# Shrunk spectra stored in six residue classes where PSUM is read, forward spectra turned on chip for every batch

## Chip, core and metric

The kernel runs on one core of a Trainium2 chip. The metric is the device time of one execution in microseconds (us), lower is better; the median over runs counts. Matrix products run on TensorE (PE; its weight loads are listed apart as PEld), element-wise work on VectorE (DVE), ScalarE (ACT) and GpSimd (POOL); SyncE (SP) issues most DMAs. [...]

## What is computed

Three parts in a row. First, for 8 batches of a sequence of 3072 rows by 256 columns, a spectral layer; then a soft mixture of 8 experts with 4 slots each over all 24576 rows; then a feed-forward layer.

```python
X = np.fft.rfft(x, axis=1)                      # 8 batches
Yr = Xr @ w_r - Xi @ w_i + b_r
Yi = Xr @ w_i + Xi @ w_r + b_i
Yr = np.sign(Yr) * np.maximum(np.abs(Yr) - 0.01, 0.0)   # "shrunk" spectra
Yi = np.sign(Yi) * np.maximum(np.abs(Yi) - 0.01, 0.0)
y = np.fft.irfft(Y, n=3072, axis=1)
...
logits = x @ phi                                # x is y, 32 slots
d = exp(logits - logits.max(0)); d /= d.sum(0) + 1e-9
slot_input = d.T @ x                            # through relu(. @ w1) @ w2 per expert
c = exp(logits - logits.max(1)); c /= c.sum(1) + 1e-9
x = c @ slot_out
...
h = x @ w_in
out = (h * tanh(softplus(h))) @ w_out
```

## The kernel before

The rows y are never formed. Since the slots are linear in y, the kernel projects the shrunk spectrum on phi, turns the 32 projected columns back by an inverse transform to get the logits, makes the weights d, transforms d forward, and sums spectrum times transformed weights. The inverse and forward transforms are split in two steps each (64 by 48 points).

The front part (up to about 645 us) works in 32 steps, four for each batch b; step k = 4b+g treats a quarter of the spectrum, all 256 channels in two halves `h` (input) or `eh` (output). In one step:

- `load_b` brings the result of the first transform step from DRAM, `stage2` does the second transform step in PSUM (tile `s`), ACT rounds it to a high part `xh`, DVE takes the low part `xl`.
- `linear` multiplies with the three weight combinations a, b, c (m = 0, 1, 2; six products each half, tile `l`). For m = 0 ACT copies PSUM to `k1`. For m = 1 and 2 (real and imaginary part) DVE adds `k1` to PSUM, giving `p`; ACT makes `cl` and overwrites `p` (two Relu with bias); POOL subtracts the two into `yt`, the shrunk spectrum. `cl` has one buffer, `p` two, `yt` two.
- `project` (tile `pp`) and `inv1` (tile `iu`) begin the logits. `ytrans` turns `yt` with 12 products against the identity (tile `tr`, with `yt` as the stationary operand), and ACT copies the result to `y`.

Once for each batch: `sturn`, `inv2` (`lps`), `smax1` to `smax3` (running maximum and exponent, tiles `mt`, `mb`, `dx`), `fwd1` (first step of the forward transform of the weights, PSUM tile `dps`, copied to `dm`), `d_load` (brings `dm` into the order that the next step wants, tile `dd`), `fwd2` (`dt`), `dturn` (`dh`), `slots` (`sps`: sum over `y` with `dh`). In `ctrans` the combine weights c are turned (`ctps`) with a contiguous operand. `stage1` (PSUM tile `s`, copied by ACT to `a`) and `store_a` prepare the batch ahead. `conv` converts the feed-forward weights in pieces on DVE and POOL.

One layout matters. Before, `yt` holds for each output half (8 q) x (real, imaginary) x (48 f), and `ytrans` takes column 2c+i and every sixth after it, six classes m in all. `dm` and `dd`: before, for all batches but the last, ACT copies `dps` to `dm`, a DMA stores it to the DRAM tile `ddr`, and a second DMA loads it as `dd` in the new order. The last batch has a second way: two DVE transposes of 32x32 blocks out of PSUM with a stepped output, eight products with the identity (`td`), and two copies out of PSUM.

The order of the work is written by hand. Every piece is put with `at(position, ...)` on one line of positions counted in steps k, and all pieces are issued in the order of positions; each engine and each DMA queue then works strictly in that order. The constants are in the table `PA` (`dl` places `d_load`, `f1` `fwd1`, `f2` `fwd2`); the last four steps and the last batch have their own table `TAIL`. The PSUM tiles of the front part share eight buffers, given out in turn. After 690 us only the feed-forward layer `ffn` runs.

Of the kernel before, what the change touches and what calls it, by code (L numbers as in the profile page):

```python
# [8 lines left out]
F32 = mybir.dt.float32  # L9
# [12 lines left out]
NP = 32  # L22
# [9 lines left out]
def constants():  # L32

    n1 = np.arange(R1, dtype=np.float64)
    n2 = np.arange(R2, dtype=np.float64)
    f1 = np.zeros((R1, R1))
    t = np.zeros((96, NP, 96))
    w = 2.0 * np.pi / SEQ
    f1[:, 0], f1[:, 1] = 1.0, np.where(n1 % 2 == 0, 1.0, -1.0)
    for pos in range(47):  # L40
        k, r = (R1 * (pos + 1), 0) if pos < 23 else (R1 // 2 + R1 * (pos - 23), R2)
        a = w * np.mod(n2 * k, SEQ)
        t[r:r + R2, 0, pos] = np.cos(a)
        t[r:r + R2, 0, 48 + pos] = -np.sin(a)
    t[0:R2, 0, 47] = 1.0
    t[0:R2, 0, 95] = np.where(n2 % 2 == 0, 1.0, -1.0)
    for q in range(1, NP):
        ang = 2.0 * np.pi * np.mod(n1 * q, R1) / R1
        f1[:, 2 * q], f1[:, 2 * q + 1] = np.cos(ang), -np.sin(ang)
        for k2 in range(R2):  # L50
            a = w * np.mod(n2 * (q + R1 * k2), SEQ)
            sg = 1.0 if k2 < R2 // 2 else -1.0
            t[0:R2, q, k2] = np.cos(a)
            t[R2:96, q, k2] = np.sin(a)
            t[0:R2, q, 48 + k2] = -sg * np.sin(a)
            t[R2:96, q, 48 + k2] = sg * np.cos(a)
    fd = np.kron(f1, np.eye(2))
    sel = np.tile(np.eye(NS), (4, 1))
    m = np.arange(128).reshape(4, 4, 2, 4)
    order = m.transpose(1, 0, 2, 3).reshape(-1)  # L60
    big = np.concatenate([fd, fd.T[order], np.eye(128), sel, np.tile(f1, (2, 1))], axis=1)
    tt = t.transpose(2, 1, 0)
    t3 = np.concatenate([t[:, :, 0:48] + t[:, :, 48:96], t], axis=2)
    both = np.concatenate([t3.reshape(96, -1), tt.reshape(96, -1)], axis=1)
    return np.ascontiguousarray(big.astype(np.float32)), np.ascontiguousarray(both.astype(np.float32))
# [3 lines left out]
def body(ctx, tc, x, w_r, w_i, b_r, b_i, phi, w1, w2, w_in, w_out, cbig, ct, out, dbg=None, stop=False):  # L69
# [154 lines left out]
    def stage2(k, h, p0):  # L224
        b, g = divmod(k, 4)
        n = min(3, 8 - p0)
        if h == 0 and p0 == 0:
            xh_t[k] = bp.tile([128, 2, 3 * NC + 48], F32R, tag="xh", name="xh")
            xl_t[k] = bp.tile([128, 2, 3 * NC + 48], F32R, tag="xl", name="xl")
        full = psum([128, 3, 3, 48], "s2")  # L230
        ps = full[:, 0:n]
        for i in range(n):
            nc.tensor.matmul(ps[:, i], lhsT=b_t[k][:, p0 + i, h * 128:(h + 1) * 128], rhs=t_m[:, 8 * g + p0 + i, :],  # L233
                             start=True, stop=True)

        def part(t):
            return t[:, h, 144 * p0:144 * (p0 + n)].rearrange("p (q r f) -> p q r f", r=3, f=48)

        xh = part(xh_t[k])
        nc.scalar.activation(out=xh, in_=ps, func=AF.Copy)  # L240
        nc.vector.tensor_sub(part(xl_t[k]), ps, xh.bitcast(F32))  # L241
        if g == 0 and p0 == 0:
            for t in (xh_t[k], xl_t[k]):
                nc.vector.tensor_copy(t[:, h, 3 * NC:3 * NC + 48].rearrange("p (a r) -> p a r", r=2),
                                      t[:, h, 95:144:48][:, None, :].to_broadcast([128, 24, 2]).bitcast(F32))

    def linear(k, eh, m):
        if eh == 0 and m == 0:
            pool, tag = (bp, "b") if k >= NK - 2 else (yq, "yq") if k >= NK - 4 else (ytp, "yt")
            yt_t[k] = pool.tile([128, 2, 8, 2, 48], F32, tag=tag, name="yt")  # L250
        xh, xl, yt = xh_t[k], xl_t[k], yt_t[k]
        src, (wh, wl) = ((0, wsp["a"]), (2, wsp["b"]), (1, wsp["c"]))[m]
        w, nq = (NC + 2, 9) if m == 0 and k % 4 == 0 else (NC, 8)
# [11 lines left out]
                nc.tensor.matmul(full[:, 0:48 * nq].rearrange("p (q f) -> p q f", f=48), lhsT=ww[:, h, es], rhs=spec(xx, h), start=n == 0, stop=n == 5)  # L265
                n += 1
        if m == 0:
            k1_t[eh] = lp.tile([128, NC + 2], F32, tag="k1", name="k1")
            nc.scalar.activation(out=k1_t[eh][:, 0:w], in_=ps, func=AF.Copy)
            if w > NC:  # L270
                cs_t[eh] = cs = sm.tile([128, 2, 2], F32, tag="cs", name="cs")
                for i, sc in ((0, 0.5), (1, -0.5)):
                    nc.scalar.activation(out=cs[:, i], in_=k1_t[eh][:, NC:w], func=AF.Relu, scale=sc, bias=half[:, i, eh:eh + 1])
            return
        ri = m - 1
        p = lp.tile([128, 8, 48], F32, tag="p", name="p")
# [697 lines left out]
```

## Time and profile before

| What | Value |
|---|---|
| three runs | 1929.86, 1931.71, 1935.7 us; median 1931.71 |
| profiled execution, own time | 1935.8 us |
| its span (first to last instruction) | 1934.0 us |
| PE busy | 1875.3 us, 97% of the span |
| DVE, ACT, POOL busy | 1163.1, 860.5, 195.3 us |
| mean DMA share up to 600 us | about 0.6 to 0.9 of the 16 engines |
| small packets (under 512 B) | 28784 of 96905 |
| chain that ended last | PE 88%, DMA 4%, DVE 3%, ACT 2%, issue 2%, POOL 1% |

The busy time of PE includes the pipelining of products, so a busy PE may still be shortened. The rows that follow come from the profiled execution; it is 4.1 us (0.2%) above the median.

### The profile page before, as it was taken

What the parts mean: (1) busy time and instruction counts of PE and PEld (TensorE: products, weight loads), DVE (VectorE), ACT (ScalarE), POOL (GpSimd) and SP (SyncE); (2) the same over time, 40 slices, a digit from 0 to 9 for tenths busy, and PEclk for the clock granted to TensorE, in tenths of its full rate; (3) what the DMA queues carried; (4) which work ended last, traced back from release to release, by engine and by line L of the source; (5) the groups of instructions that cost most, each with busy time, mean ns of one, the idle gap of its engine ahead of it and who ended that gap; (6) DMA issues with size and microseconds to landing.
All of it is one profiled execution on the core that took longest, in us unless ns stands there. A gap on an engine that the chain in (4) does not pass through costs nothing.

```text
span 1934.0 us, 29831 instructions
## 1 busy us (share of the span) xinstructions
PE 1875.3 (97%) x12106; PEld 1569.4 (81%) x12106; DVE 1163.1 (60%) x1810; ACT 860.5 (44%) x1380; POOL 195.3 (10%) x247
## 2 busy tenths in 40 slices
PE   6899999998998899999999999999999999999999
PEld 4687787777887488888888888888888888888887
DVE  3355655655566476666666666666666666666665
ACT  2666666665754243333333333333333333333332
POOL 0333333332332000000000000000000000000000
PEclk9999999999999999999999999999999999999999
DMA  9867777775663920020020020002002001000000
GB/s 246 235 150 173 168 184 177 170 185 132 161 167 107 343 74 22 23 55 22 12 55 23 23 55 23 23 12 55 22 23 55 22 19 48 22 23 22 23 22 23
DMA packets 96905, 164.28 MB, mean 85 GB/s; under 512 B 28784, under 2 KB 58096, under 8 KB 94848
## 3 DMA queue, kind: packets, MB, share of 16 engines
q1 hardware_dynamic: 93808, 155.13, 29.2%
q0 software_dynamic: 1792, 4.76, 0.8%
q10 hardware_dynamic: 1168, 2.49, 0.5%
q8 instruction: 95, 1.56, 0.3%
q14 instruction: 42, 0.34, 0.1%
HBM read 98.78 MB, written 63.57 MB: 84 GB/s over the span
## 4 chain that ended last, share of the span: by engine, by line
PE 88%; DMA 4%; DVE 3%; ACT 2%; issue 2%; POOL 1%; SPq 0%; POOLq 0%; ACTq 0%; DVEq 0%
PE o L910 56%; PE h L868 9%; PE l L265 8%; PE s L233 6%; PE tr L318 2%; PE s L201 2%; DMA dd<-ddr 2%; DMA bt<-sdr 1%; PE pp L296 1%; DMA xc<-in_x_dram 1%; PE sps L496 1%; POOL yt L285 1%; PE dt L478 1%; ACT cl L283 1%; PE iu L307 1%
## 5 line engine op out<-in xcount | busy, mean ns | idle before, releaser
L910 PE MATMUL o<-whl,gh 128*128 128x512 f32 x3072 | 1082.9, 395 | 0.0
L910 PE MATMUL o<-whl,gl 128*128 128x256 f32 x3072 | 827.9, 280 | 0.0
L881 ACT ACTIVATE g<-h 128x1024 f32<-128x1024 f32 (+1 forms) x385 | 394.2, 1025 | 747.8 <-PE h L868 738.0
L910 PEld LDWEIGHTS o<-whl,gh 128*128 128x128 f32 x3072 | 566.5, 188 | 121.5
L910 PEld LDWEIGHTS o<-whl,gl 128*128 128x128 f32 x3072 | 578.5, 188 | 31.5
L894 DVE TENSOR_TENSOR gl<-g,gh 128x1024 fp32r<-128x1024 f32 x383 | 468.9, 1224 | 29.2 <-DVE gh L887 1.4
L887 DVE CAST gh<-g 128x1024 fp32r<-128x1024 f32 (+1 forms) x385 | 265.8, 690 | 352.6 <-ACT g L881 352.6
L868 PE MATMUL h<-ctt,mst 128*128 128x512 f32 x768 | 240.7, 394 | 1.5 <-ACT g L881 1.0
L233 PE MATMUL s<-tall,bt 96*128 96x144 f32 x1024 | 143.0, 301 | 23.0 <-DMA bt<-sdr 12.1
L233 PEld LDWEIGHTS s<-tall,bt 96*128 96x128 f32 x1024 | 138.6, 202 | 31.0 <-issue 26.4
L241 DVE TENSOR_TENSOR xl<-s,xh 128x432 fp32r<-128x432 f32 (+1 forms) x192 | 94.6, 550 | 113.6 <-ACT xh L240 113.3
L285 POOL TENSOR_TENSOR yt<-cl,p 128x384 f32<-128x384 f32 x124 | 125.2, 1010 | 352.6 <-ACT p L284 220.2
L868 PEld LDWEIGHTS h<-ctt,mst 128*128 128x128 f32 x768 | 121.0, 188 | 19.7 <-ACT g L881 1.8
L283 ACT ACTIVATE cl<-p,tup 128x384 f32<-128x384 f32 x124 | 76.3, 615 | 134.0 <-DVE p L277 98.1
L918 DVE TENSOR_TENSOR os<-o,os 128x256 f32<-128x256 f32 x192 | 76.5, 419 | 77.2 <-ACT os L917 77.2
L277 DVE TENSOR_TENSOR p<-l,k 128x384 f32<-128x384 f32 x128 | 70.6, 553 | 85.2 <-PE l L265 61.9
L240 ACT ACTIVATE xh<-s 128x432 fp32r<-128x432 f32 (+1 forms) x192 | 79.0, 503 | 36.7 <-PE s L233 36.3
L917 ACT ACTIVATE os<-o 128x256 f32<-128x256 f32 x192 | 73.4, 383 | 41.5 <-PE o L910 37.7
L284 ACT ACTIVATE p<-p,tlo 128x384 f32<-128x384 f32 x124 | 76.3, 615 | 4.0
L201 PE MATMUL s<-xc,f 64*64 64x512 f32 x384 | 56.6, 650 | 9.6 <-DMA xc<-in_x_dram 9.5
L318 PEld LDWEIGHTS tr<-cb,yt 128*128 128x128 f32 x384 | 55.4, 235 | 12.0 <-issue 4.5
L318 PE MATMUL tr<-cb,yt 128*128 128x128 f32 x384 | 62.2, 306 | 0.0
(187 smaller groups left out, 1392.1 us busy)
## 6 DMA issues: line engine op xcount, KB each, us to landing
sdr<-a SPq DMA_DIRECT2D x96, 256.0 KB, 3.8
bt<-sdr SPq DMA_DIRECT2D x32, 768.0 KB, 8.5
out_dram<-os SPq DMA_DIRECT2D x47, 512.0 KB, 2.6
xc<-in_x_dram SPq DMA_DIRECT2D x90, 256.0 KB, 5.4
ctt<-c_d SPq DMA_DIRECT2D x28, 384.0 KB, 7.0
w1t<-in_moe_w_dram SPq DMA_DIRECT2D x6, 1024.0 KB, 7.4
c_d<-chl SPq DMA_DIRECT2D x14, 384.0 KB, 2.8
w2t<-in_moe_w_dram SPq DMA_DIRECT2D x5, 1024.0 KB, 12.2
```

Of the source, the lines that this page charges most:

```text
L201: nc.tensor.matmul(ps[h][64 * c:64 * c + 64], lhsT=f64[hs], rhs=t[hs, XC * c:XC * c + XC], start=True, stop=True, tile_position=(64 * h, 6 ...
L233: nc.tensor.matmul(ps[:, i], lhsT=b_t[k][:, p0 + i, h * 128:(h + 1) * 128], rhs=t_m[:, 8 * g + p0 + i, :], start=True, stop=True)
L241: nc.vector.tensor_sub(part(xl_t[k]), ps, xh.bitcast(F32))
L265: nc.tensor.matmul(full[:, 0:48 * nq].rearrange("p (q f) -> p q f", f=48), lhsT=ww[:, h, es], rhs=spec(xx, h), start=n == 0, stop=n == 5)
L283: nc.scalar.activation(out=cl, in_=p, func=AF.Relu, bias=tup[:, ri, eh:eh + 1])
L285: nc.gpsimd.tensor_sub(yt[:, eh, :, ri, :], cl, p)
L318: nc.tensor.transpose(ps[:, i, eh], yt[:, eh].rearrange("p q r f -> p (q r f)")[:, 2 * c + i::6], ident)
L868: nc.tensor.matmul(ps[:, i], lhsT=mst[:, f * 128:f * 128 + 128], rhs=ct_t[b][:, 4 * m:4 * m + 4].rearrange("p n t -> p (n t)"), start=True ...
L881: nc.scalar.activation(out=v(g), in_=v(h), func=AF.Mish)
L887: nc.vector.tensor_copy(v(gh), v(g))
L894: nc.vector.tensor_sub(gl, g, gh.bitcast(F32))
L910: nc.tensor.matmul(o, lhsT=a[:, i, ts], rhs=w, start=f == 0 and n == 0, stop=f == 15 and n == 1)
```

## The change

1. `yt` becomes [128, 2, 6 m, 128]: for each half, six blocks of 128, one for each class m, and within a block q, then real and imaginary part, then 8 f. The reordering happens where PSUM is read: `split6` views the PSUM tile with steps of 6 elements (24 bytes), and `k1`, `p` and `cl` are held in the order m, q, f. POOL writes `yt` in runs of 8 elements where it wrote runs of 48. The transposes take 128 contiguous columns; `project` reads runs of 16 instead of 32, and the rows of the constant table `tt` are permuted to match.
2. `fwd1` and `d_load` take the on-chip way in all batches; the DRAM tile and its two DMAs go. `dl` goes from 2.05 to 2.2.
3. In the first piece of each fourth step, the two special bins are spread over 48 columns from PSUM by one ACT copy and one DVE subtraction, instead of two DVE copies after the rounding. Two small Relu (`cs`) read PSUM instead of `k1`.

The title of the change also speaks of the second stage in one block; the positions of `stage2` are the same in both versions.

```diff
-    tt = t.transpose(2, 1, 0)
+    r = np.arange(16)
+    tt = t.transpose(2, 1, 0)[np.concatenate([6 * r + m for m in range(6)])]
...
         nc.scalar.activation(out=xh, in_=ps, func=AF.Copy)
+        real = g == 0 and p0 == 0
+        if real:
+            bins = full.rearrange("p q r f -> p (q r f)")[:, 95:144:48][:, None, :].to_broadcast([128, 24, 2])
+            bh, bl = (t[:, h, 3 * NC:3 * NC + 48].rearrange("p (a r) -> p a r", r=2) for t in (xh_t[k], xl_t[k]))
+            nc.scalar.activation(out=bh, in_=bins, func=AF.Copy)
         nc.vector.tensor_sub(part(xl_t[k]), ps, xh.bitcast(F32))
-        if g == 0 and p0 == 0:
-            for t in (xh_t[k], xl_t[k]):
-                nc.vector.tensor_copy(t[:, h, 3 * NC:3 * NC + 48].rearrange("p (a r) -> p a r", r=2),
-                                      t[:, h, 95:144:48][:, None, :].to_broadcast([128, 24, 2]).bitcast(F32))
+        if real:
+            nc.vector.tensor_sub(bl, bins, bh.bitcast(F32))
+
+    def split6(t):
+        return t[:, 0:NC].rearrange("p (q f m) -> p m q f", q=8, m=6)
...
-            k1_t[eh] = lp.tile([128, NC + 2], F32, tag="k1", name="k1")
-            nc.scalar.activation(out=k1_t[eh][:, 0:w], in_=ps, func=AF.Copy)
+            k1_t[eh] = lp.tile([128, 6, 8, 8], F32, tag="k1", name="k1")
+            nc.scalar.activation(out=k1_t[eh], in_=split6(full), func=AF.Copy)
...
-        p = lp.tile([128, 8, 48], F32, tag="p", name="p")
-        nc.vector.tensor_add(p.rearrange("p q f -> p (q f)"), ps, k1_t[eh][:, 0:NC])
+        o = yt[:, eh].rearrange("p m (q r f) -> p m q r f", q=8, r=2)[:, :, :, ri]
+        p = lp.tile([128, 6, 8, 8], F32, tag="p", name="p")
+        nc.vector.tensor_add(p, split6(full), k1_t[eh])
...
-            nc.gpsimd.tensor_sub(yt[:, eh, :, ri, :], cl, p)
+            nc.scalar.activation(out=cf, in_=pf, func=AF.Relu, bias=tup[:, ri, eh:eh + 1])
+            nc.scalar.activation(out=pf, in_=pf, func=AF.Relu, scale=-1.0, bias=tlo[:, ri, eh:eh + 1])
+            nc.gpsimd.tensor_sub(o, cl, p)
...
-                nc.tensor.transpose(ps[:, i, eh], yt[:, eh].rearrange("p q r f -> p (q r f)")[:, 2 * c + i::6], ident)
+                nc.tensor.transpose(ps[:, i, eh], yt[:, eh, 2 * c + i], ident)
...
-            if last:
-                nc.vector.transpose(out=dm.rearrange("p q n -> p n q")[:, 12 * i:12 * i + 12], in_=ps)
-            else:
-                nc.scalar.activation(out=dm[:, 12 * i:12 * i + 12], in_=ps, func=AF.Copy)
...
-        ddr[b] = dram.tile([NP, 96, NS], F32, tag="ddr", bufs=2, name="ddr")
-        nc.sync.dma_start(out=ddr[b].rearrange("q (r n) s -> (q r) n s", r=4), in_=dm)
+            nc.vector.transpose(out=dm.rearrange("p q n -> p n q")[:, 12 * i:12 * i + 12], in_=ps)
+        ch[b, 0] = dm
...
     def d_load(b):
         if b < NB - 1:
-            dd = cp.tile([96, NP, NS], F32, tag="dd", name="dd")
-            nc.sync.dma_start(out=dd, in_=ddr[b].rearrange("q p s -> p q s"))
-            ch[b, 0] = [dd[:, q] for q in range(NP)]
-            return
+            both = cp.tile([96, 2, 4, 128], F32, tag="dd", name="dd")
```

On PE, in the second batch between the projection and the forward transform `dt`, this stands before:

```order
L296 MATMUL pp<-yt,ph 32x256 x6
L318 MATMUL tr<-cb,yt 128x128 x12
L265 MATMUL l<-xh,ch 128x384
L265 MATMUL l<-xl,ch 128x384
L265 MATMUL l<-xh,cl 128x384
...
L201 MATMUL s_2463<-xc,f_120 64x512 x2
L201 MATMUL s_2464<-xc,f_120 64x512 x2
L478 MATMUL dt<-tall,dd 32x16x6 x8
```

and this now:

```order
L305 MATMUL pp<-yt,ph 32x256 x6
L452 MATMUL td<-cb,dm 96x128 x8
L327 MATMUL tr<-cb,yt 128x128 x12
L272 MATMUL l<-xh,ch 128x384
L272 MATMUL l<-xl,ch 128x384
L272 MATMUL l<-xh,cl 128x384
...
L202 MATMUL s_2481<-xc,f_120 64x512 x2
L202 MATMUL s_2482<-xc,f_120 64x512 x2
L477 MATMUL dt<-tall,dd 32x16x6 x8
```

Eight `td` stand ahead of the twelve `tr`; nothing else moves on PE.

On DVE, in the same batch, around the sum `p` that is made after `dps`, before:

```order
L277 TENSOR_TENSOR p<-l,k_2283 128x384
L552 SCALAR_TENSOR_TENSOR cvc<-cvs 128x256
L277 TENSOR_TENSOR p<-l,k_2283 128x384
L241 TENSOR_TENSOR xl<-s_2344,xh 128x432
L241 TENSOR_TENSOR xl<-s_2350,xh 128x432
```

and now:

```order
L285 TENSOR_TENSOR p<-l,k_2292 128x384
L551 SCALAR_TENSOR_TENSOR cvc<-cvs 128x256
L285 TENSOR_TENSOR p<-l,k_2292 128x384
L441 STREAM_TRANSPOSE dm<-dps 128x12x32 x2
L247 TENSOR_TENSOR xl<-s_2351,xh 128x432
L247 TENSOR_TENSOR xl<-s_2357,xh 128x432
```

The two transposes `dm` stand between the sums and the low parts; on ACT the two copies `dm` are gone from ahead of the copies `a` and `xh`.

On the SP queue, in the same stretch, before:

```order
L440 DMA ddr<-dm 128x768
L216 DMA sdr<-a 128x1x512 x2
L445 DMA dd<-ddr 96x32x32
L183 DMA xc<-in_x_dram 64x1024 x2
L221 DMA bt<-sdr 96x8x256
```

and now:

```order
L217 DMA sdr<-a 128x1x512 x2
L184 DMA xc<-in_x_dram 64x1024 x2
L222 DMA bt<-sdr 96x8x256
L532 DMA cvs<-in_moe_w_in_dram 128x512
L217 DMA sdr<-a 128x1x512 x2
```

The store of `dm` and the load of `dd` are gone from the queue, and the loads behind them move up.

## Rows read from the trace of the kernel before

**Rows 1.** Busy time by stretch: PE, PEld, DVE, ACT, POOL (instructions), clock, DMA.

```profile
core 0: us, PE busy (x) PEld busy (x) DVE busy (x) ACT busy (x) POOL busy (x), PEclk, DMA share, GB/s
60.00:130.00 70.00, 62.05 (x446) 48.32 (x443) 30.92 (x72) 42.36 (x86) 21.75 (x28) 0.93 0.79 205
...
203.00:276.00 73.00, 70.59 (x605) 55.61 (x604) 44.08 (x102) 48.06 (x100) 25.09 (x32) 1.00 0.71 174
...
690.00:1934.00 1244.00, 1239.97 (x6847) 1071.42 (x6845) 783.38 (x950) 457.00 (x571) 0.00 (x0) 1.00 0.09 29
```

**Rows 2.** Waits of PE, 20 to 640 us: total us, times, longest.

```profile
PE s L233 <- DMA bt<-sdr: 12.1, 3, 6.5
PE dt L478 <- DMA dd<-ddr: 9.9, 7, 2.5
...
PE s L233 <- ACT dm L435: 2.5, 5, 0.9
PE dps L431 <- ACT dx L384: 1.8, 2, 1.2
```

**Rows 3.** Chain that ended last, 200 to 300 us: start, us, what.

```profile
231.51 6.26 DMA dd<-ddr
...
256.61 0.33 PE ctps L413 x3
...
270.80 1.82 PE tr L318 x12
```

**Rows 4.** Groups by line and form: weight loads of the transposes, busy us, mean ns.

```profile
L318 PEld LDWEIGHTS tr<-cb,yt 128*128 128x128 f32 x384 | 55.4, 235 | 12.0 <-issue 4.5 <-DVE p L277 3.3 <-DVE xl L241 2.5
...
L413 PEld LDWEIGHTS ctps<-cb,lg 128*128 128x128 f32 x48 | 5.9, 147 | 1.9 <-POOL lg L405 1.5 <-issue 0.4
```

**Rows 5.** Timeline at 638 us, the last batch's on-chip turn: start, us.

```profile
638.09 1.08 PE L453 MATMUL td<-cb,dm 128*96 128x128 f32 x8
```

**Rows 6.** Groups by form: what takes `dps` and `td` out of PSUM.

```profile
L435 ACT ACTIVATE dm<-dps 128x384 f32<-128x384 f32 x14 | 5.9, 474 | 0.0
...
L433 DVE STREAM_TRANSPOSE dm<-dps 128x384 f32<-128x384 f32 x2 | 2.1, 1152 | 0.2 <-PE dps L431 0.2
...
L456 DVE COPY dd<-td 96x512 f32<-96x512 f32 x1 | 0.7, 686 | 1.2 <-PE td L453 1.2
```

**Rows 7.** Timeline around `dm` in the second batch; in brackets idle time before.

```profile
224.63 0.55 DVE L277 TENSOR_TENSOR p<-l,k 128x384 f32<-128x384 f32 x1
...
228.75 1.49 PE L233 MATMUL s<-tall,bt 96*128 96x144 f32 x10 [0.48 <-ACT dm L435]
...
230.50 2.88 DVE L241 TENSOR_TENSOR xl<-s,xh 128x432 fp32r<-128x432 f32 x6 [5.32 <-ACT xh L240]
```

**Rows 8.** Groups by form: PSUM reads, `rm` and `mst` stepped, `p` and `a` contiguous.

```profile
L277 DVE TENSOR_TENSOR p<-l,k 128x384 f32<-128x384 f32 x128 | 70.6, 553 | 85.2 <-PE l L265 61.9 <-POOL yt L285 12.7 <-POOL yt L288 4.1
...
L207 ACT ACTIVATE a<-s 128x512 f32<-128x512 f32 x90 | 48.8, 592 | 18.5 <-PE s L201 11.8 <-DMA xc<-in_x_dram 6.5
...
L343 DVE TENSOR_REDUCE rm<-lps 128x32 f32<-128x384 f32 x16 | 8.3, 553 | 13.5 <-ACT lg L341 13.4
...
L851 ACT ACTIVATE mst<-mr 128x512 fp32r<-128x512 f32 x2 | 1.1, 595 | 1.4 <-PE mr L846 1.4
```

**Rows 9.** Groups by form: element-wise work on POOL.

```profile
L285 POOL TENSOR_TENSOR yt<-cl,p 128x384 f32<-128x384 f32 x124 | 125.2, 1010 | 352.6 <-ACT p L284 220.2 <-PE tr L318 78.9 <-ACT chl L414 14.4
...
L554 POOL TENSOR_TENSOR cvc<-cva,cvc 128x256 f32<-128x256 f32 x32 | 23.3, 729 | 17.4 <-DVE cvc L552 17.4
...
L392 POOL TENSOR_TENSOR lg<-lg,cm 128x768 f32<-128x768 f32 x1 | 1.5, 1482 | 19.4 <-DVE cm L391 19.4
```

**Rows 10.** Waits of ACT, 130 to 640 us: total us, times, longest.

```profile
ACT cl L283 <- POOL yt L285: 26.1, 24, 1.5
```

**Rows 11.** Groups by form: the two DVE copies of the special bins.

```profile
L244 DVE CAST xl<-xl 128x48 fp32r<-128x48 f32 x16 | 4.0, 247 | 0.0
...
L244 DVE CAST xh<-xh 128x48 fp32r<-128x48 f32 x16 | 3.3, 204 | 0.0
```

More of the change, by code (lines that the diff above doesn't have):

```diff
@@ L125, in body @@
     x_t, b_t, xh_t, xl_t, yt_t, y_t, pt_t, k1_t = {}, {}, {}, {}, {}, {}, {}, {}
-    sdr, spt, ddr, ch, a_t = {}, {}, {}, {}, {}
+    sdr, spt, ch, a_t = {}, {}, {}, {}
     XC = 512
@@ L249, in linear @@
             pool, tag = (bp, "b") if k >= NK - 2 else (yq, "yq") if k >= NK - 4 else (ytp, "yt")
-            yt_t[k] = pool.tile([128, 2, 8, 2, 48], F32, tag=tag, name="yt")
+            yt_t[k] = pool.tile([128, 2, 6, 128], F32, tag=tag, name="yt")
         xh, xl, yt = xh_t[k], xl_t[k], yt_t[k]
@@ L272, in linear @@
                 for i, sc in ((0, 0.5), (1, -0.5)):
-                    nc.scalar.activation(out=cs[:, i], in_=k1_t[eh][:, NC:w], func=AF.Relu, scale=sc, bias=half[:, i, eh:eh + 1])
+                    nc.scalar.activation(out=cs[:, i], in_=full[:, NC:w], func=AF.Relu, scale=sc, bias=half[:, i, eh:eh + 1])
             return
         ri = m - 1
-        p = lp.tile([128, 8, 48], F32, tag="p", name="p")
-        nc.vector.tensor_add(p.rearrange("p q f -> p (q f)"), ps, k1_t[eh][:, 0:NC])
-        cl = lp.tile([128, 8, 48], F32, tag="cl", bufs=1, name="cl")
+        o = yt[:, eh].rearrange("p m (q r f) -> p m q r f", q=8, r=2)[:, :, :, ri]
+        p = lp.tile([128, 6, 8, 8], F32, tag="p", name="p")
+        nc.vector.tensor_add(p, split6(full), k1_t[eh])
+        cl = lp.tile([128, 6, 8, 8], F32, tag="cl", bufs=1, name="cl")
+        pf, cf = (t.rearrange("p m q f -> p (m q f)") for t in (p, cl))
         if k == NK - 1:
-            nc.vector.tensor_scalar(cl, p, tlo[:, ri, eh:eh + 1], thi[:, ri, eh:eh + 1], op0=ALU.max, op1=ALU.min)
-            nc.vector.tensor_sub(yt[:, eh, :, ri, :], p, cl)
-        else:
-            nc.scalar.activation(out=cl, in_=p, func=AF.Relu, bias=tup[:, ri, eh:eh + 1])
-            nc.scalar.activation(out=p, in_=p, func=AF.Relu, scale=-1.0, bias=tlo[:, ri, eh:eh + 1])
-            nc.gpsimd.tensor_sub(yt[:, eh, :, ri, :], cl, p)
+            nc.vector.tensor_scalar(cf, pf, tlo[:, ri, eh:eh + 1], thi[:, ri, eh:eh + 1], op0=ALU.max, op1=ALU.min)
+            nc.vector.tensor_sub(o, p, cl)
+        else:
+            nc.scalar.activation(out=cf, in_=pf, func=AF.Relu, bias=tup[:, ri, eh:eh + 1])
+            nc.scalar.activation(out=pf, in_=pf, func=AF.Relu, scale=-1.0, bias=tlo[:, ri, eh:eh + 1])
+            nc.gpsimd.tensor_sub(o, cl, p)
         if m == 2 and k % 4 == 0:
             cs = cs_t.pop(eh)
-            nc.gpsimd.tensor_sub(yt[:, eh, 0, :, 47], cs[:, 0], cs[:, 1])
+            nc.gpsimd.tensor_sub(yt[:, eh, 5, 7:16:8], cs[:, 0], cs[:, 1])
     def project(k):
@@ L293, in project @@
         for eh in range(2):
-            v = yt[:, eh].rearrange("p q r f -> p q (r f)")
+            v = yt[:, eh].rearrange("p m (q j) -> p q m j", q=8)
             for a in range(3):
-                nc.tensor.matmul(ps[32 * a:32 * a + 32], lhsT=ph[:, eh, :], rhs=v[:, :, 32 * a:32 * a + 32],
+                nc.tensor.matmul(ps[32 * a:32 * a + 32], lhsT=ph[:, eh, :], rhs=v[:, :, 2 * a:2 * a + 2],
                                  start=eh == 0, stop=eh == 1, tile_position=(0, 32 * a))
@@ L427, in fwd1 @@
         last = b == NB - 1
-        dm = cp.tile([128, 32, N2] if last else [128, N2, NS], F32, tag="st" if last else "chl", bufs=1 if last else 2, name="dm")
+        dm = cp.tile([128, 32, N2], F32, tag="st" if last else "chl", bufs=1 if last else 2, name="dm")
         for i in range(2):
@@ L431, in fwd1 @@
             nc.tensor.matmul(ps, lhsT=f1, rhs=d[:, 12 * i:12 * i + 12], start=True, stop=True)
-            if last:
-                nc.vector.transpose(out=dm.rearrange("p q n -> p n q")[:, 12 * i:12 * i + 12], in_=ps)
-            else:
-                nc.scalar.activation(out=dm[:, 12 * i:12 * i + 12], in_=ps, func=AF.Copy)
-        if last:
-            ch[b, 0] = dm
-            return
-        ddr[b] = dram.tile([NP, 96, NS], F32, tag="ddr", bufs=2, name="ddr")
-        nc.sync.dma_start(out=ddr[b].rearrange("q (r n) s -> (q r) n s", r=4), in_=dm)
+            nc.vector.transpose(out=dm.rearrange("p q n -> p n q")[:, 12 * i:12 * i + 12], in_=ps)
+        ch[b, 0] = dm
     def d_load(b):
         if b < NB - 1:
-            dd = cp.tile([96, NP, NS], F32, tag="dd", name="dd")
-            nc.sync.dma_start(out=dd, in_=ddr[b].rearrange("q p s -> p q s"))
-            ch[b, 0] = [dd[:, q] for q in range(NP)]
-            return
+            both = cp.tile([96, 2, 4, 128], F32, tag="dd", name="dd")
         src = ch[b, 0].rearrange("p (c r) n -> p c (r n)", r=4)
@@ L453, in d_load @@
                 nc.tensor.transpose(ps[:, c], src[:, 4 * a + c], ident)
-            dd = yp.tile([96, 4, 128], F32, tag="y", name="dd")
+            dd = both[:, a] if b < NB - 1 else yp.tile([96, 4, 128], F32, tag="y", name="dd")
             if a:
@@ L795, in run @@
                 nc.vector.tensor_copy(sot[:, h, 16 * g:16 * g + 16].rearrange("p (j i) -> p j i", i=SPE), src)
-PA = dict(y=20, s1=-5.89, s1d=0.3402, lb=-1.91, s2=-1.1, s2d=0.0002, pj=1.18, yt=2.24, ytd=0.0002, tu=0.482, i2=1.17, m1=1.17, m2=1.34, m3=1.51, f1=1.84, c1=1.58, ce=1.58, ds=2.47, dl=2.05, c2=2.57, f2=2.46, sl=3.2, rc=0.3, cx=3.24, cxd=0.0002, x0=-0.79, x1=0.05, ytl=1.05, x2=1.3, x3=2.7)
+PA = dict(y=20, s1=-5.89, s1d=0.3402, lb=-1.91, s2=-1.1, s2d=0.0002, pj=1.18, yt=2.24, ytd=0.0002, tu=0.482, i2=1.17, m1=1.17, m2=1.34, m3=1.51, f1=1.84, c1=1.58, ce=1.58, ds=2.47, dl=2.2, c2=2.57, f2=2.46, sl=3.2, rc=0.3, cx=3.24, cxd=0.0002, x0=-0.79, x1=0.05, ytl=1.05, x2=1.3, x3=2.7)
 TAIL = {
```

## Prediction

> **What bounds the kernel now.** I read the busy time by stretch first [rows 1]. After 690 us PE is busy 1240.0 of 1244 us with the feed-forward layer, which the change does not touch; all gain or loss lies before that. In a typical stretch of the front part (203 to 276 us, about one batch) PE is busy 70.6 of 73 us, DVE 44.1, ACT 48.1, POOL 25.1, the DMA engines 71%. So the front part too is bound by PE, and what counts is PE's own work and the few microseconds in which it waits. From 60 to 130 us it is not so: PE is idle 8 us there, and the longest wait for a load of `bt`, 6.5 us [rows 2], falls in it; work saved there is partly lost again.
>
> Next come the waits of PE [rows 2]. Two of the four matter here: `dt` waits 7 times, 9.9 us in all, for the load of `dd`, and `stage2` waits 5 times, 2.5 us, until ACT has copied `dm` and so freed a PSUM buffer. The first load of `bt` (12.1 us, three times) is early and untouched. `dps` waits 1.8 us for the exponent.
>
> Then the chain that ended last [rows 3]. It shows the load of `dd` with 6.26 us in that batch, and on PE a group of twelve `tr` in 1.82 us, 0.152 us each. Three `ctps`, the same 128x128 transpose but with a contiguous operand, take 0.33 us, 0.110 us each. The weight loads say where the difference sits: 235 ns for the stepped `yt`, 147 ns for the contiguous operand [rows 4].
>
> **The change part by part.**
>
> *Transposes with contiguous operands.* 32 steps with 12 each: 384 transposes, from 0.152 to 0.110 us by the rows of [rows 3], 12 x 0.042 = 0.50 us a step. The lower bound is no gain at all, if the 0.152 is not due to the step of 24 bytes; the upper is 32 x 0.50 = 16 us. The row nearest in kind, same engine, same shape, same stretch, is `ctps`, so I take 0.110. The first three steps' transposes run where PE is idle for loads anyhow [rows 1]; 29 x 0.50 = **-14.5 us**.
>
> *No trip of `dm` through DRAM.* The wait of `dt` goes, **-9.9 us** [rows 2]. What is late next: `dd` now needs `td` and two copies. After `td` PE still has twelve `tr`, six `l` and four products of `stage1` ahead of `dt`, about 3.4 us, and the copies take 0.69 us on DVE [rows 6] and 0.59 us on ACT (the 128x512 copy `a` of [rows 8] is the same length), so `dt` should not wait. The wait of `stage2` for `dm` goes too, **-2.5 us** [rows 2], if DVE empties `dps` earlier than ACT did. In the second batch DVE ends its sum `p` at 225.18 us [rows 7]; two transposes of 1152 ns [rows 6] end at 227.5 us, and the product that waited stands at 228.75 us [rows 7]. So yes, with about 1.2 us to spare.
>
> *What the on-chip turn costs.* PE gets eight `td` in each of seven batches. In the last batch eight took 1.08 us [rows 5]; bounds are 8 x 0.10 = 0.8 and 1.1 us, I take 1.0: **+7.0 us**, all on the path since PE is the bound. DVE gets 2 x 1.152 + 0.69 = 3.0 us a batch and ACT loses 2 x 0.474 and gains 0.59 us [rows 6, 8]. Behind the DVE transposes stand the six low parts `xl`, and PE waits for those before the next `linear`. They are hidden: DVE was idle 5.32 us before `xl`, waiting for ACT [rows 7]. Without that cover 7 x 2.3 = 16 us of `xl` would come late. ACT reaches `a` and `xh` some 0.9 us earlier. On the SP queue 14 issues go and `bt` is issued earlier; past 130 us PE waits for no `bt`, so I count nothing.
>
> *The chain of the softmax moves up less than PE does.* From `inv2` to `dps` there is a latency chain over DVE and ACT, and PE already waits 1.8 us at its end [rows 2]. Each batch PE has one group of `tr` less by 0.5 us in this stretch; where `dps` waits, that gain is lost. Bounds 0 and 7 x 0.5 = 3.5 us, I take **+2 us**.
>
> *Reading PSUM in steps of 24 bytes.* 128 sums `p` on DVE and 64 copies `k1` on ACT. The trace shows no read with this step, but two others. `rm` reads 384 elements of PSUM in steps of 128 bytes in 553 ns, as `p` reads its 384 contiguously in 553; `mst` reads 512 elements on ACT in steps of 16 bytes in 595 ns, and `a` contiguously in 592 [rows 8]. So nothing, as the near value. The other bound is what steps cost on the writing side: `dm`, 384 elements written in steps of 96 bytes, takes 1152 ns [rows 6], 0.6 us more than `p`.
> [...]
>
> *POOL's writes in runs of 8.* `yt` takes 1010 ns for 384 elements in runs of 48. From 256 and 768 elements (729 and 1482 ns) comes 1.47 ns an element and 353 ns fixed, 918 ns for 384 [rows 9]. The 92 ns above it are either 8 runs at 11.5 ns, and 48 runs would make 1.47 us, or not a price of runs at all; the 768-element row, whose third operand repeats in 24 runs, shows none. Bounds 0 and +0.46 us each; I take 0.1. POOL is idle two thirds of the time, but it sends back `cl` and `p`: ACT waited 24 times, 26.1 us, for it [rows 10], and behind ACT's `cl` stand the PSUM copies that PE needs. **+1 us**.
>
> *The special bins.* DVE loses 16 pairs of copies (204 + 247 ns [rows 11]) and gains 16 subtractions, ACT gains 16 copies of 48 columns; bounds of each by the same rows, 0.2 and 0.3 us. Two for each batch, hidden by DVE's and ACT's free third; if not hidden, 16 x 0.3 = 5 us. I take 0. The two small Relu that now read PSUM hold a buffer a little longer, and the permuted rows of `tt` and `project`'s runs of 16 change no count; 0.
>
> The sum: -14.5 - 9.9 - 2.5 + 7.0 + 2 + 1 = -16.9 us, from the profiled execution's own 1935.8 to 1918.9. That execution was 4.1 us above the median of 1931.7; taken from the median, **1915 us**.
>
> **The rivals.**
>
> A. The 0.152 us of a transpose is not the step. Then only the way of `dm` counts: -16.9 + 14.5 = -2.4, 1929 us. Against it: the 88 ns in the weight load [rows 4].
>
> B. POOL pays for short runs, +0.46 us each. ACT's two `cl` between `dps` and `xh` come late by it in each of seven batches, 7 x 2 x 0.46 = 6.4 us, and about seven `yt` of the last steps, where the chain passes through POOL, add 3.2: +10 less the 1 already in, 1924 us. For it: the 92 ns. Against: POOL's idle time.
>
> C, slower. The stepped PSUM reads cost what the stepped write costs, 0.6 us. Of each step's work two sums stand ahead of `xl` on DVE, and PE's next products need `xl`: 2 x 0.6 x 32 = 38 us on the path, -17 + 38 = +21, 1953 us. It decides from 17 / 64 = 0.27 us a read. Against it: [rows 8]. For it: no row has this step.
>
> D. More gain: the relief of ACT reaches PE. ACT worked without a break in the stretch around `dps`; with 0.95 us less of `dm` there, PE gains 7 x 0.9 = 6.3 instead of 2.5, the softmax chain comes no later (2), and the first steps' transposes count as well (1.5), and POOL costs nothing (1): -25, 1907 us.
>
> **How the numbers follow.** Chances: forecast 0.60 (its own range 1908 to 1923), A 0.08, B 0.12, C 0.09, D 0.11. Three runs of this kernel spread by 0.3%, so 0.3%, 5.8 us, is about what can be told from no change: below 1926 is faster, above 1937.5 slower. Faster gets the forecast, D, and about half of B (others of it come out nearer to nothing), 0.77; slower C, 0.09; the rest, 0.14, is the same. The range reaches down past D to 1900 and up past A to 1930; outside are C and a part of the edges.
>
> **What would show it.** After: twelve `tr` in about 1.3 us and their weight loads near 147 ns; no `dd` from DRAM, and no wait of `dt` over half a microsecond; eight `td` in about 1 us; `p` near 553 ns; `yt` near 1.1 us on POOL; DVE some 47 of 73 us a batch, and the feed-forward layer beginning 17 us earlier. I am wrong if `p` or `k1` are much longer, if `xl` comes late behind `dm`, or if the transposes keep their pace.

## The result and the profile after

The changed kernel takes 1908.14 us (median of 4 runs, 1907.59 to 1910.2) against 1931.36 (4 runs, 1929.86 to 1935.7): ratio 0.9878, 95% interval 0.9861 to 0.9896, so 1.2% faster. Its profiled execution took 1908.3 us, 27.5 less than the one of before; by the medians it is 23.2 less, since the profiled execution of before lay 4.4 us above the median of its four runs.

The busy time by stretch (columns as in [rows 1]):

```profile
60.00:130.00 70.00, 60.93 (x451) 46.82 (x444) 30.87 (x69) 42.39 (x88) 21.32 (x27) 0.93 0.79 206
...
203.00:276.00 73.00, 71.82 (x627) 57.31 (x626) 45.91 (x101) 50.35 (x107) 26.25 (x33) 1.00 0.64 166
...
422.00:495.00 73.00, 73.00 (x644) 58.28 (x639) 46.90 (x106) 50.66 (x108) 24.91 (x32) 1.00 0.67 165
```

PE is busy 71.8 to 73 of 73 us, at a granted clock of 1.00. The waits of PE, 120 to 610 us:

```profile
PE dps L440 <- ACT dx L393: 2.5, 3, 1.2
PE pp L305 <- POOL yt L294: 2.2, 2, 1.6
PE mt L364 <- DVE rm L359: 2.2, 2, 1.6
PE dt L477 <- ACT dd L457: 0.9, 1, 0.9
```

The waits for `dd` and `dm` of [rows 2], and those for `bt` in this stretch, are gone; only `dt` of the seventh batch, the last but one, waits 0.9 us. Instead the latency chain of the softmax shows (`dps`, `mt`, and `pp` for POOL's last `yt`). The chain that ended last, 200 to 300 us, has the groups that answer to [rows 3]:

```profile
227.28 1.01 PE td L452 x8
228.29 1.31 PE tr L327 x12
...
249.50 0.33 PE ctps L422 x3
...
264.35 1.46 PE tr L327 x12
```

And the groups by line and form:

```profile
L294 POOL TENSOR_TENSOR yt<-cl,p 128x384 f32<-128x384 f32 x124 | 125.8, 1014 | 321.8 <-ACT p L293 196.2 <-ACT y L332 40.4 <-DVE chl L424 31.3
...
L285 DVE TENSOR_TENSOR p<-l,k 128x384 f32<-128x384 f32 x128 | 70.5, 552 | 70.4 <-PE l L272 46.1 <-POOL yt L294 10.2 <-POOL yt L297 4.1
...
L327 PEld LDWEIGHTS tr<-cb,yt 128*128 128x128 f32 x384 | 42.2, 141 | 9.6 <-issue 4.7 <-DVE p L285 3.3 <-DVE cvs L549 0.8
...
L276 ACT ACTIVATE k<-l 128x384 f32<-128x384 f32 x64 | 32.3, 505 | 10.3 <-PE l L272 9.9
...
L441 DVE STREAM_TRANSPOSE dm<-dps 128x384 f32<-128x384 f32 x16 | 16.7, 1149 | 0.2 <-PE dps L440 0.2
```

The weight load of a transpose fell from 235 to 141 ns; `p` reads PSUM in steps of 24 bytes in 552 ns (553 before); POOL's `yt` in runs of 8 takes 1014 ns (1010).

### The profile page after: what moved, and what is told of

Its sections match the earlier page's. It is cut to its first block, busy times and chain, and to the rows that moved or that the text cites. A ratio compares the mean times of both kernels' runs of the same rounds, so it can differ in the third digit from the quotient of the medians.

```text
span 1906.5 us, 29946 instructions
## 1 busy us (share of the span) xinstructions
PE 1860.7 (98%) x12162; PEld 1555.7 (82%) x12162; DVE 1179.5 (62%) x1815; ACT 854.4 (45%) x1389; POOL 196.5 (10%) x247
## 4 chain that ended last, share of the span: by engine, by line
PE 90%; DVE 3%; ACT 2%; issue 2%; DMA 1%; POOL 1%; SPq 0%; POOLq 0%; ACTq 0%; DVEq 0%
PE o L909 56%; PE h L867 9%; PE l L272 8%; PE s L234 6%; PE s L202 2%; PE tr L327 2%; PE pp L305 1%; PE sps L495 1%; POOL yt L294 1%; PE dt L477 1%; DVE xl L247 1%; DMA xc<-in_x_dram 1%; PE iu L316 1%; PE dps L440 0%; ACT cl L292 0%
## 5 line engine op out<-in xcount | busy, mean ns | idle before, releaser
L294 POOL TENSOR_TENSOR yt<-cl,p 128x384 f32<-128x384 f32 x124 | 125.8, 1014 | 321.8 <-ACT p L293 196.2
L234 PE MATMUL s<-tall,bt 96*128 96x144 f32 x1024 | 135.7, 292 | 15.5 <-DMA bt<-sdr 8.4
L234 PEld LDWEIGHTS s<-tall,bt 96*128 96x128 f32 x1024 | 133.0, 195 | 21.4 <-issue 20.2
L241 ACT ACTIVATE xh<-s 128x432 fp32r<-128x432 f32 (+1 forms) x192 | 78.7, 501 | 29.4 <-PE s L234 28.8
L332 ACT ACTIVATE y<-tr 128x512 f32<-128x512 f32 x93 | 50.1, 600 | 16.1 <-PE tr L327 16.1
L208 ACT ACTIVATE a<-s 128x512 f32<-128x512 f32 x90 | 49.1, 597 | 16.8 <-PE s L202 8.4
```

The source lines that it names most:

```text
L294: nc.gpsimd.tensor_sub(o, cl, p)
```

## What the prediction had left out, seen in the profile of before

The terms of the sum explain 17 us. Going back to the profile of before with the new trace beside it, two things stand out that the new one does not have. First, the granted clock by stretches of 10 us (columns as in [rows 1]):

```profile
390.00:400.00 10.00, 9.64 (x62) 8.17 (x66) 4.55 (x13) 5.71 (x11) 2.31 (x4) 0.83 0.51 126
460.00:470.00 10.00, 6.72 (x76) 5.64 (x74) 5.10 (x12) 2.95 (x5) 3.26 (x4) 0.85 1.00 262
470.00:480.00 10.00, 10.00 (x73) 8.13 (x76) 5.06 (x15) 5.11 (x11) 0.00 (x0) 0.81 0.37 85
```

In these three the granted clock is 0.81 to 0.85; in the changed kernel it is 1.00 in every such stretch from 110 to 610 us. Second, PE's timeline there:

```profile
390.36 5.83 PE L233 MATMUL s<-tall,bt 96*128 96x144 f32 x32 [2.38 <-DMA bt<-sdr]
...
461.23 0.87 PE L478 MATMUL dt<-tall,dd 96*32 96x96 f32 x32
...
468.36 6.83 PE L233 MATMUL s<-tall,bt 96*128 96x144 f32 x32 [3.28 <-DMA bt<-sdr]
...
537.41 0.54 PE L478 MATMUL dt<-tall,dd 96*32 96x96 f32 x16 [1.62 <-DMA dd<-ddr]
...
540.07 1.51 PE L478 MATMUL dt<-tall,dd 96*32 96x96 f32 x32
...
544.66 4.08 PE L233 MATMUL s<-tall,bt 96*128 96x144 f32 x32
...
605.28 0.54 PE L478 MATMUL dt<-tall,dd 96*32 96x96 f32 x16 [2.53 <-DMA dd<-ddr]
...
607.61 1.51 PE L478 MATMUL dt<-tall,dd 96*32 96x96 f32 x32
```

The 32 products of `stage2` take 5.83 and 6.83 us after a wait for `bt`; without a wait, at 544.66 us, the same group takes 4.08 us. So two of the three waits for `bt` in [rows 2] (5.7 us) lie not early but here, and after both PE runs slow, 4.5 us in all. It also runs slow after two of the seven waits of `dt` for `dd`: there the middle group of `dt` takes 1.51 instead of 0.87 us, and with the products around it each stretch is about 1.5 us longer (worked out from the starts). That makes some 7.5 us of PE's work. For comparing runs I use a rougher measure below, the *clock loss*: the sum over the stretches of 10 us from 110 to 610 us of (1 - granted clock) x 10 us, in the one profiled execution. It is 8.3 us before and 0.0 after; it counts also the part of a lower clock that falls into a wait of PE, where it costs nothing.

## The experiments

Two theories at first. W: only the wait of `dt` for `dd` counted. Q: the trip through DRAM also held up the SP queue, so that `bt` came late, PE waited, and the clock fell.

| Kernel | Ratio to before, 95% interval | PE waits for `dd`, `bt`, us | Clock loss, us | Mean granted clock, all executions |
|---|---|---|---|---|
| before | 1 | 9.9, 5.7 | 8.3 | 0.9912 |
| changed | 0.9878, 0.9861 to 0.9896 | 0.9, 0 | 0.0 | 0.9940 |
| changed_again | 0.9869, 0.9852 to 0.9886 | 0.9, 0 | 1.7 | 0.9938 |
| layout_alone | 0.9981, 0.9966 to 0.9995 | 13.0, 3.2 | 6.8 | 0.9895 |
| turn_alone | 0.9920, 0.9897 to 0.9943 | 0.9, 0 | 0.0 | 0.9943 |
| dummy_trip | 0.9888, 0.9868 to 0.9908 | 0.9, 0.8 | 0.0 | 0.9938 |
| trip_on_act_queue | 1.0059, 1.0039 to 1.0079 | 18.3, 0 | 10.2 | 0.9878 |
| before_late_dt | 1.0051, 1.0035 to 1.0067 | 0, 11.9 | 17.0 | 0.9870 |
| layout_late_dt | 1.0037, 1.0022 to 1.0052 | 0.5, 16.6 | 20.4 | 0.9849 |
| td_doubled | 0.9900, 0.9887 to 0.9913 | 0, 0 | 1.7 | 0.9942 |
| td_late | 0.9969, 0.9957 to 0.9981 | 14.0, 0 | 6.8 | 0.9900 |
| bt_first | 1.0078, 1.0058 to 1.0098 | 28.8, 0 | 20.4 | 0.9840 |
| bt_first_dt_later | 1.0035, 1.0021 to 1.0048 | 17.9, 0 | 15.4 | 0.9870 |
| trip_early | 0.9861, 0.9837 to 0.9884 | 0, 2.2 | 0.0 | 0.9933 |

(Waits from 120 to 610 us, and clock loss, in the one profiled execution of each kernel. Under `dd` also the wait for its last copy out of PSUM, where the turn is on chip; in bt_first_dt_later a further wait of `dt`, 3.8 us, is put down to DVE. The last column is the mean over a whole execution, and over all executions on record: 55 of the kernel before.)

**layout_alone.** The changed kernel with `fwd1`, `d_load` and `dl` of before:

```diff
-            nc.vector.transpose(out=dm.rearrange("p q n -> p n q")[:, 12 * i:12 * i + 12], in_=ps)
+            nc.scalar.activation(out=dm[:, 12 * i:12 * i + 12], in_=ps, func=AF.Copy)
...
+        nc.sync.dma_start(out=ddr[b].rearrange("q (r n) s -> (q r) n s", r=4), in_=dm)
...
+            nc.sync.dma_start(out=dd, in_=ddr[b].rearrange("q p s -> p q s"))
```

> The changed layout of yt and the special bins, with the trip of dm through DRAM and its place as before. The sum of the prediction gives its transposes 14.5 us and takes 1 us back: 13.5 us less than before. Theory Q (the trip through DRAM also holds up the SP queue, so that bt comes late, PE waits, and the granted clock falls after such waits): the trip is still there, so these waits stay, and a part of the 14.5 us runs into the waits for dd and bt, which grow; 7 to 11 us less than before. Theory W (only the wait of dt for dd counted, the queue did not): 12 to 14 us less, with the wait of dt somewhat longer.

Only 0.2%, 3.7 us: less than either theory said. The transposes were faster, but PE waited 13.0 instead of 9.9 us for `dd` (and 3.2 instead of 5.7 for `bt`), and the clock was lower: 0.9895 over 12 executions against 0.9915 over the 17 of before on the same chip, by an estimate from the difference, 0.0020 x 1930, some 4 us.

**turn_alone.** The kernel before with `fwd1`, `d_load` and `dl` of the changed one.

> The on-chip turn of the forward spectra in all batches, with yt, its transposes and the special bins as before. By the prediction's terms -9.9 - 2.5 + 7.0 + 0 to 2: 3 to 5 us less than before. Theory Q: besides these, no wait for bt after 130 us and no fall of the granted clock between 120 and 620 us; 10 to 14 us less. Theory W: 3 to 6 us less, and the waits for bt remain.

0.8%, 15.5 us, a little more than Q's 10 to 14 and far from W: no waits for `dd` or `bt`, no clock loss. So the larger part of the gain comes with the turn, although its own terms in the sum are only 5.4 us.

**dummy_trip.** The changed kernel plus the old store and load, read by nobody.

```diff
+            nc.sync.dma_start(out=ddr[b].rearrange("q (r n) s -> (q r) (n s)", r=4), in_=dm.rearrange("p q n -> p (q n)"))
...
+            nc.sync.dma_start(out=dz, in_=ddr[b].rearrange("q p s -> p q s"))
```

> The changed kernel, which in seven batches also issues the old store of dm to DRAM and the old load on the SP queue at their old places (positions 1.84 and 2.05); the loaded tile is read by nobody, so no engine waits for it. It computes the same. Theory Q: SP waits in its queue for dm and for the landing of the store, the small packets slow the other loads, bt comes late again: 5 to 12 us more than the changed kernel. Theory W: nobody waits for the load, so within 2 us of the changed kernel.

Against Q: 0.9888, not to be told from the changed kernel. Its SP queue in the second batch (`dps` begins at 218.38 us):

```profile
222.79 0.33 SPq L445 DMA_DIRECT2D ddr<-dm  x1
224.91 1.20 SPq L217 DMA_DIRECT2D sdr<-a  x2
226.19 0.63 SPq L450 DMA_DIRECT2D dz<-ddr  x1
226.91 3.68 SPq L184 DMA_DIRECT2D xc<-in_x_dram  x2
230.70 0.52 SPq L222 DMA_DIRECT2D bt<-sdr  x1
```

and of the kernel before (`dps` begins at 222.80 us):

```profile
229.10 0.33 SPq L440 DMA_DIRECT2D ddr<-dm  x1
230.07 1.20 SPq L216 DMA_DIRECT2D sdr<-a  x2
231.51 0.48 SPq L445 DMA_DIRECT2D dd<-ddr  x1
232.09 3.71 SPq L183 DMA_DIRECT2D xc<-in_x_dram  x2
235.90 0.53 SPq L221 DMA_DIRECT2D bt<-sdr  x1
```

and of the changed kernel (`dps` begins at 217.46 us):

```profile
225.29 1.67 SPq L184 DMA_DIRECT2D xc<-in_x_dram  x2
...
228.27 0.33 SPq L222 DMA_DIRECT2D bt<-sdr  x1
```

With the trip, in both kernels, the two `xc` behind its load take 3.7 us to issue (1.67 in the changed kernel), and `bt` stands behind them. But before, `bt` is issued 13.1 us after `dps` begins, with the dummy 12.3, and in the changed kernel 10.8. It lands 7.4 to 7.9 us later, that is 21.0, 19.9 and 18.2 us after `dps`; `stage2` begins at 21.1, 20.0 and 19.9. So the changed kernel has 1.7 us to spare, and the other two 0.1; before, that is so only because PE has already waited for `dd`. In three other batches of the dummy `stage2` waits 0.8 to 0.9 us and begins 0.1 us after `bt` has landed; the profile puts one of these waits down to `bt`.

**trip_on_act_queue.** The kernel before; store and load issued by `nc.scalar`.

> The kernel before, with the store of dm and the load of dd issued by ACT instead of SP, at the same places in the program. Theory Q: SP no longer waits for dm and for the store, bt is issued earlier, its waits after 130 us go: 4 to 10 us less than before, though dt still waits for dd. Theory W: dt waits as before, so no more than 2 us from the kernel before.

Against both: slower. `bt` is issued earlier (12.4 us after `dps` in the second batch) and nobody waits for it; but the load of `dd` now takes 7.7 us to land instead of 6.2, with `xc` and `bt` beside it, and `dt` waits 18.3 us for it.

A second pair of theories. V: any wait of PE costs more than its length, because of the clock. R: the trip itself slows the rest.

**before_late_dt.** The kernel before, one line:

```diff
-ds=2.47, dl=2.05, c2=2.57, f2=2.46
+ds=2.71, dl=2.05, c2=2.57, f2=2.7
```

> The kernel before with only the place of the forward transform dt changed (f2 from 2.46 to 2.70, and ds, which reads its result, to 2.71), so that PE reaches dt about 2.5 us of its own work later; the trip through DRAM stays on the SP queue. Theory V (the waits of PE for dd cost more than their length, since the granted clock is at its lower level for some microseconds after them): no wait of dt for dd, no fall of the clock from 110 to 610 us, hardly a wait for bt; 9.9 + 8.3 = 18 us less than before by its profile, 12 to 20. Rival R (the trip itself, its small packets and its place in the queue, slows the rest): only the waits go, 6 to 10 us less, and the clock still falls or bt still comes late.

**layout_late_dt.** The same shift on layout_alone.

> The changed layout and bins with the trip through DRAM kept, and dt placed at 2.70. Theory V: the gain of the transposes that layout_alone lost in waits comes out whole, and the seven groups of td (7 us of PE) are not paid: 3 to 7 us less than the changed kernel, no fall of the clock. Rival R: the trip still costs, so the changed kernel is the faster one by 0 to 8 us.

Both missed, in sign: slower than before. The waits of PE in before_late_dt:

```profile
PE s L233 <- DMA bt<-sdr: 11.9, 5, 3.6
```

`dt` no longer waits, so PE arrives earlier at `stage2` and waits there for the `bt` that was queued behind `dd`, with more clock loss than before (17.0 us). V had counted the gain and not what comes next in the queue.

**td_doubled.** Every `td` product made twice, in seven batches.

```diff
+            if b < NB - 1:
+                for c in range(4):
+                    nc.tensor.transpose(ps[:, c], src[:, 4 * a + c], ident)
```

> The changed kernel with every td product of the first seven batches made twice (the second overwrites the first, the result is the same). Prices td where PE is the bound: 7 x 1.0 = 7 us more than the changed kernel, 5.5 to 8; if the products hide in idle time of PE, under 3.

0.9900, against 0.9878 and 0.9869 for the changed kernel: 2.2 to 3.1 thousandths, 4 to 6 us, though the intervals overlap with the first of the two; the profiled spans differ by 2.8 and 6.5 us (1913.0 against 1910.2 and 1906.5). At or under the low end of the expectation: most of the turn's products are on the path.

**td_late.** `dl` from 2.2 to 2.455.

> The changed kernel with td right ahead of dt (dl from 2.2 to 2.455), so that PE waits in each of seven batches for the two copies of dd, with no DMA in it: about 1.5 us each, 10 us. Theory V: the clock falls after these waits as it did after those for the DMA, 13 to 22 us more than the changed kernel. If the fall belongs to the DMA or to bt and not to PE's wait: 7 to 12 us more and a full clock from 110 to 610 us.

0.9969 against 0.9869 to 0.9878: 18 to 19 us more, in V's range, and no DMA in the wait. The timeline of PE at one of the waits:

```profile
310.64 0.62 PE L477 MATMUL dt<-tall,dd 96*32 96x96 f32 x16 [2.04 <-ACT dd L457]
...
311.83 0.69 PE L272 MATMUL l<-xh,ah 128*128 128x384 f32 x1
312.31 0.52 PE L272 MATMUL l<-xl,ah 128*128 128x384 f32 x1
...
315.26 0.34 PE L272 MATMUL l<-xl,bh 128*128 128x384 f32 x1
```

After 2.04 us of idleness the same product takes 0.52 us (granted clock 0.83 from 310 to 320 us), and 0.34 again three microseconds later. Waits of 14.0 us and a clock loss of 6.8 us make 20.8; the time rose by 18 to 19. Not every wait did this: of the seven, PE's clock fell after four (of the 6.8 us of clock loss 1.7 are from 310 to 320 us).

**bt_first.** layout_late_dt with `dl` 2.10, so that `bt` stands ahead of `dd`. V2 and R2 are V and R with the queue in the account.

> layout_late_dt with one more shift: dl from 2.05 to 2.10, so that on the SP queue the load of bt stands ahead of the load of dd instead of behind it. Theory V2 (before and layout_late_dt pay for whichever load ends last, dd or the bt queued behind it, and for the lower clock after the wait): the waits for bt, 16.6 us in layout_late_dt, go nearly to nothing; dt, 2.5 us later than at first, waits for dd by 0 to 2 us a batch; 15 to 30 us less than layout_late_dt. Rival R2 (the trip's bytes and small packets slow all loads, in whatever order): bt still waits over 8 us, less than 8 us gained.

**bt_first_dt_later.** `f2` 2.85, `ds` 2.86, `sl` 3.35 besides.

> As bt_first, with dt at 2.85 (ds 2.86, the sums over the slots at 3.35), some 4 us more of PE's own work ahead of most of dt. Theory V2: no wait of dt, hardly one for bt, a full clock from 110 to 610 us, and no td on PE: 0 to 6 us less than the changed kernel. Rival R2: more than the changed kernel by 10 us or over.

Both kernels are slower than before. The first half of V2 came true, no wait for `bt` at all; the second did not. By the times alone R2 was right twice, but not by its reason, since `bt` came in time. The load of `dd`, now behind `bt`, took 8.4 and 8.7 us to land, and `dt` waited 28.8 and 17.9 us. Turning the order round hands the wait to the other load.

**changed_again.**

> The changed kernel once more, on the same chip as the two above, for a direct comparison: 0.988 of the kernel before, by either theory.

0.9869, as expected.

**trip_early.** The trip kept, but started early:

```diff
-                nc.scalar.activation(out=dm[:, 12 * i:12 * i + 12], in_=ps, func=AF.Copy)
+                nc.vector.tensor_copy(dm[:, 12 * i:12 * i + 12], ps)
...
-dl=2.05
+dl=1.9
```

> The changed layout and bins with the trip through DRAM kept, but early: DVE instead of ACT copies dps to dm (contiguous, two copies), and dl goes from 2.05 to 1.90, so that the load of dd stands right behind its store on the SP queue; dt stays at 2.46. Theory L (in the kernel before, ACT's copies come late, some 6 us after dps begins, so that dd and the bt queued behind it both land after PE needs them; in dummy_trip DVE emptied dps 2 us earlier and the same trip cost almost nothing): no wait of dt for dd over 1 us, no wait of stage2 for dm, waits for bt under 6 us in all; no td, so 0.985 to 0.990 of the kernel before, level with the changed kernel or up to 4 us either side. Rival R2 (the trip's transfer alone is too much for this stretch): waits for bt of 10 us and more with a falling clock, 0.995 of the kernel before or slower.

0.9861, 1904.3 us median of 6 runs. Its SP queue (`dps` begins at 216.19 us):

```profile
219.53 0.33 SPq L449 DMA_DIRECT2D ddr<-dm  x1
221.99 0.33 SPq L454 DMA_DIRECT2D dd<-ddr  x1
222.71 2.89 SPq L217 DMA_DIRECT2D sdr<-a  x2
225.69 1.80 SPq L184 DMA_DIRECT2D xc<-in_x_dram  x2
228.69 0.33 SPq L222 DMA_DIRECT2D bt<-sdr  x1
```

The load of `dd` is issued 5.8 us after `dps` (8.7 before) and lands in 4.7 us, 6.3 before (medians of seven: 4.4 and 6.2); `bt` follows at 12.5. With the trip, and without a single `td`, the kernel is as fast as the changed one: the intervals overlap, so neither is shown to be the faster. This decides for L and against R2. Its two edits were not tried apart. The trace says that `dl` alone could not have done it: before, the store lands 8.6 us after `dps` and the load goes out at 8.7, so the load could not go earlier while `dm` came from ACT that late. How much DVE's copies alone would give stays open.

## Why the prediction was right, and where it was not

The direction and the range held (1915 forecast, 1908 measured), but the sum came out 6 us short of the medians, and 1908.14 stands at the very edge of the forecast's own 1908 to 1923. That it stands inside is partly luck: some 15 us that the sum left out were made up for in part by 5 us too much for the transposes, and in part because most executions of before lose less than the profiled one.

- *Transposes*, -14.5: the mechanism was right, the size too large. A group of twelve went from 1.82 to 1.46 us, 0.36 and not 0.50. I had divided the group's whole time, with its start, by 12, and compared it with `ctps` inside a running chain. That the first three groups bring nothing was right: the third starts at 122.04 us before and 121.83 after. The groups behind it give 9.7 us. And by layout_alone the whole layout is worth 3.7 us so long as the trip stays late; the prediction had "no gain at all" as a bound only for the case that the step did not matter, and not because later waits and a lower clock could take the gain back.
- *The wait of `dt`*, -9.9: gone to 0.9, and *the wait for `dm`*, -2.5: gone. DVE did empty `dps` early, at 221.86 us for a `dps` that began at 217.46.
- *`td`*, +7.0: eight took 1.01 us, 0.9 from their start to the next product's, so 6.3; td_doubled gave 4 to 6.
- *Softmax chain*, +2: `dps`, `mt` and `pp` wait 6.9 us where before the same work, to 640 us, waited 3.9 us: +3.
- *PSUM in steps*, 0, and *POOL*, +1: `p` 552 against 553 ns, `k1` 505 against 503, `yt` 1014 against 1010; all nothing. The reads of PSUM by DVE (`p`) and ACT (`k1`), now in steps of 24 bytes, take as long as the contiguous ones before. Rivals B and C fall. The step did have a price in the weight load of the transposes: 235 ns from `yt` in steps of 24 bytes, 141 ns from contiguous columns.
- *Rival A* falls with the 141 ns. *Rival D* named almost the measured time, but its mechanism did not give it: the waits behind ACT that it priced were 2.5 us in all.
- **The step that failed** is "The first load of `bt` (12.1 us, three times) is early and untouched", with "past 130 us PE waits for no `bt`, so I count nothing". One of the three waits was early; the other two, 5.7 us, stood in the stretch that the change touches, and went. The sum also priced every wait at its own length. Behind the two waits for `bt` PE's products took 4.5 us longer at the lower clock, behind two of those for `dd` about 3.0, and the sum has no term for either.

Counted on PE from the third group of `tr` to the first of the last batch (622.12 us before, 594.61 after), by the starts of its products in the two profiled executions: the waits give -9.0 - 5.7 - 2.5 + 2.8 = -14.4, `tr` -9.7, `td` +6.3, and all other products, which are the same in both kernels, -9.6; in all -27.4 of the 27.5 us. Of the 9.6 the lower clock shown above is 7.5; the other 2 us are not explained.

The profiled execution of before lost more to the clock than most. The record has the mean granted clock of every execution: of the 55 of the kernel before, two at 0.995 took 1925 and 1928 us, two at 0.988 took 1940 and 1941. Their mean is 0.9912, that of eight of the changed kernel 0.9939; an estimate from the difference, 0.0027 x 1930, is 5 us. So of the 23 to 25 us by the ratios some 5 are the clock, and the rest is waits and products. At the changed kernel's clock, 0.993 to 0.995, the kernel before still takes 1925 to 1933 us.

So the gain has two parts, and the loads decide over both. With the loads in time the layout is worth some 8 us (turn_alone 0.9920, changed 0.9878), with the trip late 3.7. The 15.5 us of the turn are not a gain of its products, which cost 4 to 6 us: trip_early reaches the same time without them. The kernel before ran two loads, `dd` and the `bt` queued behind it, into PE with nothing to spare. In the five kernels that moved only `dt`, the queue or the order of the two loads, one of them came late (11.9 to 28.8 us of waits). Starting earlier, or not going to DRAM, freed both (waits for `dd` and `bt` of 0 and 2.2 us in trip_early, 0.9 and 0 in the changed kernel). In every kernel here that is faster than before by more than layout_alone, DVE empties `dps`; a kernel that starts the trip early with ACT's copies was not tried.

## What to carry to other kernels

When a wait on a load is removed, look at what stands behind that load in its queue and how many microseconds before its use it lands: the gain is only as large as the next margin (in before_late_dt 9.9 us of waits for `dd` went, and those for `bt` grew from 5.7 to 11.9 us). Price a wait of PE with what follows it: if the profile shows a lower granted clock behind the waits, the products there at their longer duration belong to the wait (here 4.5 us behind 5.7 us of waits for `bt`). Before a trip through DRAM is replaced by work on the bound engine, try to start it earlier (trip_early 0.9861, the changed kernel 0.9878).

## Not expected of the hardware

- With the store of `dm` and a load of 3072 pieces of 128 bytes added (dummy_trip), the two transfers behind the load on the SP queue took 3.7 us to issue in the second batch, 1.67 in the changed kernel.
- In td_late a wait of 2.04 us on PE was followed by some microseconds at a lower clock (granted clock 0.83 from 310 to 320 us), where a product took 0.52 instead of 0.34 us. Not every wait did this: in the kernel before the clock fell after one of 1.62 us for `dd` (0.93 from 530 to 540 us, 0.90 from 540 to 550) and stayed at 1.00 after one of 2.24 us (160 to 180 us).
- The same load of `dd` landed in 4.4 us when it was issued ahead of `sdr` and `xc` (trip_early), 6.2 in the old place and 8.4 to 8.7 behind `bt` (medians).
